# One PSUM bank for the last 64 columns of two token tiles

## The chip, the core and the metric

The kernel runs on one core of a Trainium2 chip. Its engines each work through a queue of their own: PE (TensorE, matmuls and turns, with its weight loads, PEld, shown apart), DVE (VectorE), ACT (ScalarE), POOL (GpSimd) and SP (SyncE, which here only starts DMAs). Matmuls write to PSUM, of which the kernel has eight banks of 128 partitions by 512 fp32 values. The metric is the device time of one execution in microseconds (us).

## What is computed

With B = 1, 2048 tokens, D = 576 channels, 128 states and a hidden width of 4608:

```python
xn = layernorm(x)                                # over the 576 channels
K  = Re(sum_n C[d,n] * exp(dt*A[d,n]*l) * dt*B[d,n])   # for l = 0..2047
y  = causal_conv(xn, K) + xn * Dskip             # by FFT in the reference
h  = silu(xn @ w1)                               # 576 -> 4608
out = x + y + h @ w2                             # 4608 -> 576
```

The feed-forward part (the two large products) and the convolution part share only `xn` and the final sum.

## The kernel before

**Tiles and staging.** The tokens are 16 tiles of 128. For the first product the channels must lie on partitions, so tiles 0 to 7 are turned on PE; tiles 8 to 15 are turned through DVE and memory instead. Four tiles make a block of 512 tokens. The product's accuracy comes from splitting each operand into a rounded part and the rest: a cast on ACT gives the high part, a subtraction on DVE the rest. A turned block is held as `xh` and `xl` (channels 0 to 511, four groups of 128) and `x4`, which holds the high part of channels 512 to 575 on partitions 0 to 63 and their rest on partitions 64 to 127.

**The turn of one tile** is `put_xt`. Four turns of 128x128 fill a PSUM bank `pt` (L124), one ACT cast makes `xh` (L125), one DVE subtraction `xl` (L126). Then a second bank is taken: one turn of the last 64 columns (L128), an ACT cast of 64x128 into the upper half of `x4` (L129), a DVE subtraction into its lower half (L130). The banks come from the pool `pss`, which has three and is shared with all of the convolution's work.

**Order of the feed-forward.** `up` makes one 128-wide slice of the hidden layer for 512 tokens: twelve matmuls with `xh` and `xl` (L314), and two with `x4` (L315, L316), into one of the two banks of `ps1`; then SiLU (L322) and a cast (L323) on ACT and a subtraction (L324) on DVE. `down` multiplies four such slices by `w2` into `po` (L339), and DVE adds the result to `acc` (L343). The first block's slices are made in two halves of 256 tokens: the first after tiles 0 and 1, the second after tiles 2 and 3. Weights are loaded by SP and split like the rest (L281 and L283 for `w1`, L300 and L302 for `w2`).

**Order of the side work.** `phase0` loads, normalizes and turns tiles 0 and 1 one by one, 2 and 3, 4 and 5, 6 and 7 as pairs. `norm` takes statistics (L187, L188), an inverse root on POOL (L192) and scales on DVE (L196) or ACT (L201). `late` does tiles 8 to 15 in a buffer that the next pair reuses: after normalizing (`xj`), DVE turns 32x32 blocks (L240), SP writes them (L244), and SP writes `xj` itself to `dxn` (L245). Then come the convolution's parameters (`natural`, with three changes of the activation table on ACT), its kernel, its transforms, and at the end its sum into the output.

**What sets the order on an engine.** The program is traced in the order of the code, and a planner then orders each engine's queue by estimated times, trace order and free banks; that order is fixed before the kernel runs. `behind(pins[...])` forces instructions traced inside it to stand behind the named one on the same engine. Of the pins, `xt_h` is the last large cast, `xt_s` the last cast into `x4`, `xt_v` the last subtraction into `x4`, and `pt` the last short turn. `xt0s` (tile 0) and `xt1s` (tile 1) hold back the first casts of `w1`; `xt1`, `xt3` and `xt7` hold back DVE work behind the named tile's last subtraction; the first `w2` casts stand behind `xt_s`. While PE waits for tiles 0 and 1, it runs filler matmuls (`idle`, L858, eight after tile 0 and three after tile 1), pinned behind `pt`.

Of the kernel before, what the change touches and what calls it, by code (L numbers as in the profile page):

```python
# [19 lines left out]
P = 128  # L20
L = 2048
D = 576
# [3 lines left out]
NKT = 4  # L26
# [17 lines left out]
def kernel(  # L44
# [21 lines left out]
    nc = tc.nc  # L66
# [23 lines left out]
    ident = cst.tile([P, P], F32, name="ident")  # L90
# [23 lines left out]
    def new_xt(blk):  # L114
        xh = xtp.tile([P, NKT, 512], F32R, tag="xh", name=f"xh_{blk}")
        xl = xtp.tile([P, NKT, 512], F32R, tag="xl", name=f"xl_{blk}")
        x4 = xtp.tile([P, 512], F32R, tag="x4", name=f"x4_{blk}")
        return xh, xl, x4

    def put_xt(xh, xl, x4, src):  # L120

        pt = pss.tile([P, NKT, P], F32, tag="pss", name="pt")
        for kt in range(NKT):
            nc.tensor.transpose(pt[:, kt, :], src[:, kt * P:(kt + 1) * P], ident)  # L124
        pins["xt_h"] = nc.scalar.copy(xh, pt).ins  # L125
        nc.vector.tensor_sub(xl, pt, xh)  # L126
        pt = pss.tile([P, 512], F32, tag="pss", name="pt4")
        pins["pt"] = nc.tensor.transpose(pt[:64, :P], src[:, NKT * P:D], ident).ins  # L128
        pins["xt_s"] = nc.scalar.copy(x4[:64, :], pt[:64, :P]).ins  # L129
        pins["xt_v"] = nc.vector.tensor_sub(x4[64:, :], pt[:64, :P], x4[:64, :]).ins  # L130

    xts = {}
    pairs = {}
    pins = {}

    def behind(ins):
        return tc.issue_after(ins) if ins is not None else nullcontext()
# [24 lines left out]
    def load_x(j, pool, tag, engines):  # L162

        t = pool.tile([P, 2, D], F32, tag=tag, name=f"{tag}{j}")
        for i in range(2 if j == 0 else 1):
            for ps, v, eng in quarters(xv, engines):
                if j:
                    eng.dma_start(t[ps], v[:, j:j + 2])
                else:
                    eng.dma_start(t[ps, i], v[:, i])  # L170
        pairs[j] = t
        return t[:, 0, :], t[:, 1, :]
# [7 lines left out]
    def norm(p0, js, xs):  # L180

        n = len(js)
        st = p0.tile([P, 2, 2, 6], F32, tag="st", name="st")
        mv = p0.tile([P, 2, 2], F32, tag="mv", name="mv")
        for i in range(n):
            for h in range(2):
                nc.vector.bn_stats(out=st[:, i, h, :], in_=xs[i][:, h * HD:(h + 1) * HD])  # L187
            nc.vector.bn_aggr(out=mv[:, i, :], in_=st[:, i, :, :])  # L188
        sd = p0.tile([P, 2], F32, tag="sd", name="sd")
        mb = p0.tile([P, 2], F32, tag="mb", name="mb")  # L190
        pins["sdv"] = nc.vector.tensor_scalar(sd[:, :n], mv[:, :n, 1], 1e-5, None, op0=ALU.add).ins
        pins["sd"] = nc.gpsimd.tensor_tensor(sd[:, :n], sd[:, :n], mhalf[:, :n], op=ALU.pow).ins  # L192
        xn = p0.tile([P, 2, D], F32, tag="xn", name="xn") if js[0] < 8 else pairs[js[0]]
        for i, j in enumerate(js):
            if j % 2 == 0 or j < 4:
                pins["xn"] = nc.vector.tensor_scalar(xn[:, i, :], xs[i], mv[:, i, 0:1], sd[:, i:i + 1],  # L196
                                                 op0=ALU.subtract, op1=ALU.mult).ins
            else:
                nc.vector.scalar_tensor_tensor(mb[:, i:i + 1], mv[:, i, 0:1], -1.0, sd[:, i:i + 1],
                                               op0=ALU.mult, op1=ALU.mult)  # L200
                nc.scalar.activation(xn[:, i, :], xs[i], AF.Identity,  # L201
                                     scale=sd[:, i:i + 1], bias=mb[:, i:i + 1])
        return xn

    def phase0(p0, js, idle=None):

        xs = load_x(js[0], accp, "acc", (nc.sync, nc.scalar) if js[0] < 2 else (nc.sync,))
        acc.update(zip(js, xs))
        yield
        if js[0]:  # L210
            with behind(pins["w1l"] if js[0] == 2 else None):
                normed(p0, js, xs)
        else:
            for j, xj in zip(js, xs):
                with behind(pins["xn"] if j else None):
                    normed(p0, (j,), (xj,))
                if not j:
                    pins["xt0s"] = pins["xt_s"]
                with behind(pins["pt"]):
                    idle(3 if j else 8)  # L220
        pins[f"xt{js[1]}h"] = pins["xt_h"]
        pins[f"xt{js[1]}"], pins[f"xt{js[1]}s"] = pins["xt_v"], pins["xt_s"]
        yield

    def normed(p0, js, xs):
        xn = norm(p0, js, xs)
        for i, j in enumerate(js):
            b, jj = divmod(j, 4)
            if b < 2:
                if jj == 0:  # L230
                    xts[b] = new_xt(b)
                c = slice(jj * P, (jj + 1) * P)
                xh, xl, x4 = xts[b]
                put_xt(xh[:, :, c], xl[:, :, c], x4[:, c], xn[:, i, :])
        if js[0] >= 8:

            b, jj = divmod(js[0], 4)
            tr = p0.tile([P, 2, D], F32, tag="tr", name="tr")
            for i in range(2):
                nc.vector.transpose(tr[:, i, :], xn[:, i, :])  # L240
            for q in range(4):
                cols = dxt[b - 2][:, jj * P:(jj + 2) * P].rearrange("(k r) (i q c) -> q r i k c", r=32, i=2, q=4)[q]
                for i in range(2):
                    nc.sync.dma_start(cols[:, i], tr[32 * q:32 * q + 32, i].rearrange("r (k c) -> r k c", c=32))  # L244
        nc.sync.dma_start(dxn[:, js[0]:js[0] + len(js)], xn[:, :len(js)])  # L245
# [596 lines left out]
    def side():  # L842
# [3 lines left out]
        with tc.tile_pool(name="kf", bufs=1) as kfp:  # L846
            for n in ("f", "phi"):
                kf[n] = kfp.tile([P, D], F32, name=n + "T")
            with tc.tile_pool(name="par", bufs=1) as par:
                with tc.tile_pool(name="pa", bufs=4) as pa:  # L850

                    zero = pa.tile([P, 512], BF16, name="zero", bufs=1)
                    nc.vector.memset(zero, 0.0)
                    pz = ps1.tile([P, 512], F32, tag="ps1", name="pz")

                    def idle(n):
                        for _ in range(n):
                            nc.tensor.matmul(pz, zero[:, :P], zero, start=True, stop=True)  # L858

                    idle(12)  # L860
                    p01, p23 = phase0(pa, (0, 1), idle), phase0(pa, (2, 3))
                    next(p01)
                    yield 0
                    next(p23)
                    next(p01)
                    yield 0
                    yield 0
                    next(p23)
                    yield 0
                    for js in ((4, 5), (6, 7)):  # L870
                        with behind(pins["xt3" if js[0] == 4 else "w2l"]):
                            for _ in phase0(pa, js):
                                pass
                    kf["dt"] = steps()
                    for n, ap in (("are", a_re), ("aim", a_im)):
                        kf[n] = par.tile([96, 6, NS], F32, tag=n, name=n)
                        nc.sync.dma_start(kf[n], ap.rearrange("(p t) n -> p t n", t=6))
                    yield 0
                with tc.tile_pool(name="nat", bufs=1) as nat, tc.tile_pool(name="pb", bufs=1) as pb:
                    nt = natural(nat, par)  # L880
                    def late(j):

                        xs = load_x(j, pb, "xj", (nc.sync,))
                        yield
                        with behind(pins["xn" if j == 8 else "gl"]):
                            normed(pb, (j, j + 1), xs)
                        yield

                    tiles = chain.from_iterable(late(j) for j in range(8, NJ, 2))
                    for at, todo in ((0.0, nt), (0.0, tiles), (0.004, tiles), (0.005, tiles), (gate_of(0), nt), (0.026, tiles), (0.028, tiles), (0.036, tiles), (0.038, tiles), (gate_of(1), nt), (0.06, tiles), (gate_of(2), nt), (0.09, nt)):  # L890
                        yield at
                        with behind(pins["gl"] if at else pins["xt7"] if todo is nt else None):
                            next(todo, None)
# [108 lines left out]
```

## Time and profile before

| | |
|---|---|
| time, median of 3 runs | 1112.2 us (1112.11 to 1112.43) |
| profiled execution, its own time | 1112.55 us |
| its span in the profile | 1110.8 us |
| granted TensorE clock | 0.999 |
| busy: PE, weight loads, DVE, ACT | 1103.5, 998.1, 917.3, 708.0 us |
| turned tiles: first and last short turn (L128) | 7.36 and 42.31 us |

In rows of the profile, `L128` is a line of the kernel, `pt<-ident,xn` names what is written and read, and `x8` is a count. A timeline row begins with start and duration in us; brackets give the idle time before it and what ended it. In rows of groups the busy time and the mean duration in ns follow the first bar. The chain that ended last is followed back from the last instruction, at each step to what released it; its rows have start, duration, engine, tile and line. A PE record's end is modelled, and records of successive matmuls overlap.

### The profile page before, as it was taken

Reading aid. Unit: us, or ns where it says so; the run is one execution under the profiler, and the core shown is the slowest. Engines: PE = TensorE matmul, PEld = TensorE weight load, DVE = VectorE, ACT = ScalarE, POOL = GpSimd, SP = SyncE. Lnnn points to the kernel's source line nnn. Section 1 sums busy time; section 2 is a strip of 40 time slices with the busy share of each in tenths; the row PEclk is TensorE's granted clock in tenths of the full one; section 3 lists DMA queues with packets and bytes.
Section 4 is the critical chain, followed back from the end, with each engine's and each line's share of the span. In section 5 each row is a group of like instructions: output and inputs, shape, how many; then the busy total and the mean of one; then the engine's idle time right before and its main releaser. Section 6 shows DMA issues by size and latency. Waiting matters only on the chain.

```text
span 1110.8 us, 22919 instructions
## 1 busy us (share of the span) xinstructions
PE 1103.5 (99%) x9167; PEld 998.1 (90%) x9167; DVE 917.3 (83%) x1546; ACT 708.0 (64%) x1227; POOL 70.8 (6%) x127
## 2 busy tenths in 40 slices
PE   9999999999999999999999999999999999999998
PEld 6888999899889899899989989999999999999887
DVE  7799899999999999999999837787778778784433
ACT  4574456676777676677866536877777778774210
POOL 1101000000000000011000000000000000000111
PEclk9999999999999999999999999999999999999999
DMA  9745521425242515255834163554544445434973
GB/s 255 204 123 152 140 69 61 120 65 128 82 107 81 133 61 131 76 158 155 217 124 105 44 177 102 168 158 129 161 143 151 140 147 169 131 107 129 255 207 86
DMA packets 175851, 148.56 MB, mean 134 GB/s; under 512 B 111088, under 2 KB 142720, under 8 KB 175616
## 3 DMA queue, kind: packets, MB, share of 16 engines
q1 hardware_dynamic: 165408, 112.69, 38.0%
q0 software_dynamic: 9504, 33.49, 9.4%
q8 instruction: 72, 1.18, 0.5%
q10 hardware_dynamic: 832, 0.92, 0.3%
q14 instruction: 35, 0.29, 0.1%
HBM read 102.53 MB, written 44.61 MB: 132 GB/s over the span
## 4 chain that ended last, share of the span: by engine, by line
PE 94%; DMA 2%; DVE 1%; ACT 1%; SPq 1%; issue 0%; POOL 0%; DVEq 0%; ACTq 0%
PE po L339 40%; PE ph L314 34%; PE kp L675 3%; PE ph L315 3%; PE ph L316 3%; PE pu L805 2%; PE pb L805 2%; PE pk L805 2%; PE z L690 2%; PE pu L155 1%; PE py L826 1%; PE pu L156 1%; DMA acc<-in_A_u_dram 1%; DMA dxn<-xj 1%; DMA w1r<-in_B_w_dram 0%; DMA xj<-in_A_u_dram 0%
## 5 line engine op out<-in xcount | busy, mean ns | idle before, releaser
L339 PE MATMUL po<-w2l,gh 128*128 128x288 f32 x1152 | 339.3, 296 | 0.0
L339 PE MATMUL po<-w2h,gl 128*128 128x288 f32 x1152 | 336.9, 295 | 0.0
L339 PE MATMUL po<-w2h,gh 128*128 128x288 f32 x1152 | 336.1, 296 | 0.0
L339 PEld LDWEIGHTS po<-w2h,gh 128*128 128x128 f32 x1152 | 215.3, 188 | 7.5 <-issue 2.8
L339 PEld LDWEIGHTS po<-w2l,gh 128*128 128x128 f32 x1152 | 216.2, 188 | 5.1 <-issue 0.5
L339 PEld LDWEIGHTS po<-w2h,gl 128*128 128x128 f32 x1152 | 215.7, 188 | 0.8
L322 ACT ACTIVATE gf<-ph 128x512 f32<-128x512 f32 (+1 forms) x148 | 86.3, 584 | 142.8 <-PE ph L316 133.6
L314 PE MATMUL ph<-xh,w1h 128*128 128x512 f32 (+1 forms) x592 | 161.8, 388 | 0.7 <-ACT xh L125 0.6
L314 PE MATMUL ph<-xl,w1h 128*128 128x512 f32 (+1 forms) x592 | 161.7, 386 | 0.2 <-DVE xl L126 0.2
L314 PE MATMUL ph<-xh,w1l 128*128 128x512 f32 (+1 forms) x592 | 161.2, 386 | 0.6 <-DVE w1l L283 0.6
L343 DVE TENSOR_TENSOR acc<-po,acc 128x288 f32<-128x288 f32 x288 | 126.4, 451 | 37.8 <-PE po L339 36.3
L324 DVE TENSOR_TENSOR gl<-gf,gh 128x512 fp32r<-128x512 f32 (+1 forms) x148 | 99.0, 672 | 64.3 <-ACT gh L323 63.5
L314 PEld LDWEIGHTS ph<-xh,w1l 128*128 128x128 f32 x592 | 108.1, 188 | 20.9 <-DVE w1l L283 1.1
L314 PEld LDWEIGHTS ph<-xl,w1h 128*128 128x128 f32 x592 | 108.1, 188 | 20.5 <-DVE xl L126 0.7
L314 PEld LDWEIGHTS ph<-xh,w1h 128*128 128x128 f32 x592 | 104.5, 188 | 17.8 <-ACT xh L125 1.2
L323 ACT CAST gh<-gf 128x512 fp32r<-128x512 f32 (+1 forms) x148 | 89.5, 608 | 10.1 <-PE po L339 7.2
L632 ACT ACTIVATE c<-th,magic 128x1040 f32<-128x1040 f32 x36 | 42.1, 1169 | 37.8 <-DVE C L655 27.9
L634 ACT ACTIVATE c<-th 128x1040 f32<-128x1040 f32 x36 | 38.7, 1075 | 33.9 <-DVE th L633 33.8
L300 ACT CAST w2h<-w2r 128x576 fp32r<-128x576 f32 x72 | 47.0, 671 | 17.3 <-PE po L339 14.9
L283 DVE TENSOR_TENSOR w1l<-w1r,w1h 128x640 fp32r<-128x640 f32 x72 | 57.0, 817 | 0.2
L316 PE MATMUL ph<-x,w1l 128*128 128x512 f32 (+1 forms) x148 | 57.0, 386 | 0.0
L315 PE MATMUL ph<-x,w1h 128*128 128x512 f32 (+1 forms) x148 | 57.0, 385 | 0.0
(182 smaller groups left out, 1830.4 us busy)
## 6 DMA issues: line engine op xcount, KB each, us to landing
w2r<-in_B_w_dram SPq DMA_DIRECT2D x72, 288.0 KB, 3.9
w1r<-in_B_w_dram SPq DMA_DIRECT2D x35, 512.0 KB, 3.7
d1u<-u POOLq DMA_DIRECT2D x32, 288.0 KB, 2.4
d1k<-stage SPq DMA_DIRECT2D x18, 512.0 KB, 6.9
ur<-d1u SPq DMA_DIRECT2D x32, 288.0 KB, 3.9
kr<-d1k SPq DMA_DIRECT2D x32, 288.0 KB, 2.7
d<-yo POOLq DMA_DIRECT2D x32, 288.0 KB, 3.2
ys<-d SPq DMA_DIRECT2D x32, 288.0 KB, 11.3
```

The source lines that it names most:

```text
L283: pins["w1l"] = nc.vector.tensor_sub(l1, src, h1).ins
L300: pins["w2h"] = nc.scalar.copy(h2, r2).ins
L314: nc.tensor.matmul(ph, w[:, kt, :], v[:, kt, a:e], start=n + kt == 0, stop=False)
L315: nc.tensor.matmul(ph, h1[:, 4, :], x4[:, a:e], start=False, stop=False)
L316: pins["pe"] = nc.tensor.matmul(ph, l1[:, 4, :], x4[:, a:e], start=False, stop=True).ins
L322: nc.scalar.activation(gf, ph, AF.Silu)
L323: pins["gh"] = nc.scalar.copy(gh, gf).ins
L324: pins["gl"] = nc.vector.tensor_sub(gl, gf, gh).ins
L339: pins["pe"] = nc.tensor.matmul(po[:, :HD], G[blk, t][g][:, js], W2[half, c, t][w][:, hs], start=n == 0, stop=n == 3 * FT - 1).ins
L343: nc.vector.tensor_add(acc[j][:, hs], po[:, :HD], acc[j][:, hs])
L632: nc.scalar.activation(c65, th, AF.Identity, bias=magic)
L805: nc.tensor.matmul(dst, st, mv[:, hs], start=n == 0, stop=n == 3 * len(terms) - 1)
```

## The change

`put_xt` loses its second half. A new function `put_x4` turns the last 64 columns of two tiles into one bank, side by side, and then makes one cast and one subtraction of 64x256 for both. `normed` keeps the tiles in a list and calls `put_x4` after each odd tile, so tile 0's short turn follows tile 1's large ones, and likewise for 2 and 3, 4 and 5, 6 and 7. The pin `pt` now also names a large turn (for the eight fillers after tile 0), and `xt0s` names tile 0's large cast.

```diff
-    def put_xt(xh, xl, x4, src):
+    def put_xt(xh, xl, src):
         pt = pss.tile([P, NKT, P], F32, tag="pss", name="pt")
         for kt in range(NKT):
-            nc.tensor.transpose(pt[:, kt, :], src[:, kt * P:(kt + 1) * P], ident)
+            pins["pt"] = nc.tensor.transpose(pt[:, kt, :], src[:, kt * P:(kt + 1) * P], ident).ins
         pins["xt_h"] = nc.scalar.copy(xh, pt).ins
         nc.vector.tensor_sub(xl, pt, xh)
+
+    def put_x4(x4, srcs):
         pt = pss.tile([P, 512], F32, tag="pss", name="pt4")
-        pins["pt"] = nc.tensor.transpose(pt[:64, :P], src[:, NKT * P:D], ident).ins
-        pins["xt_s"] = nc.scalar.copy(x4[:64, :], pt[:64, :P]).ins
-        pins["xt_v"] = nc.vector.tensor_sub(x4[64:, :], pt[:64, :P], x4[:64, :]).ins
+        for i, src in enumerate(srcs):
+            pins["pt"] = nc.tensor.transpose(pt[:64, i * P:(i + 1) * P], src[:, NKT * P:D], ident).ins
+        pins["xt_s"] = nc.scalar.copy(x4[:64, :], pt[:64, :2 * P]).ins
+        pins["xt_v"] = nc.vector.tensor_sub(x4[64:, :], pt[:64, :2 * P], x4[:64, :]).ins
...
                 if not j:
-                    pins["xt0s"] = pins["xt_s"]
+                    pins["xt0s"] = pins["xt_h"]
...
-                put_xt(xh[:, :, c], xl[:, :, c], x4[:, c], xn[:, i, :])
+                put_xt(xh[:, :, c], xl[:, :, c], xn[:, i, :])
+                lasts.append(xn[:, i, :])
+                if jj % 2:
+                    put_x4(x4[:, (jj - 1) * P:(jj + 1) * P], lasts)
+                    lasts.clear()
```

More of the change, by code (lines that the diff above doesn't have):

```diff
@@ L118, in new_xt @@
         return xh, xl, x4
-    def put_xt(xh, xl, x4, src):
+    def put_xt(xh, xl, src):
         pt = pss.tile([P, NKT, P], F32, tag="pss", name="pt")
         for kt in range(NKT):
-            nc.tensor.transpose(pt[:, kt, :], src[:, kt * P:(kt + 1) * P], ident)
+            pins["pt"] = nc.tensor.transpose(pt[:, kt, :], src[:, kt * P:(kt + 1) * P], ident).ins
         pins["xt_h"] = nc.scalar.copy(xh, pt).ins
         nc.vector.tensor_sub(xl, pt, xh)
+    def put_x4(x4, srcs):
         pt = pss.tile([P, 512], F32, tag="pss", name="pt4")
-        pins["pt"] = nc.tensor.transpose(pt[:64, :P], src[:, NKT * P:D], ident).ins
-        pins["xt_s"] = nc.scalar.copy(x4[:64, :], pt[:64, :P]).ins
-        pins["xt_v"] = nc.vector.tensor_sub(x4[64:, :], pt[:64, :P], x4[:64, :]).ins
+        for i, src in enumerate(srcs):
+            pins["pt"] = nc.tensor.transpose(pt[:64, i * P:(i + 1) * P], src[:, NKT * P:D], ident).ins
+        pins["xt_s"] = nc.scalar.copy(x4[:64, :], pt[:64, :2 * P]).ins
+        pins["xt_v"] = nc.vector.tensor_sub(x4[64:, :], pt[:64, :2 * P], x4[:64, :]).ins
     xts = {}
     pairs = {}
+    lasts = []
     pins = {}
```

## The prediction

> **What bounds the kernel now.** I read the page's busy shares and the chain that ended last first, then the waits of PE, then the chain in order of time, then the timelines of PE, DVE and ACT in the first 75 us. The change lives between 6 and 44 us.
>
> ```profile
> PE 1103.5 (99%) x9167; PEld 998.1 (90%) x9167; DVE 917.3 (83%) x1546; ACT 708.0 (64%) x1227; POOL 70.8 (6%) x127
> PE 94%; DMA 2%; DVE 1%; ACT 1%; SPq 1%; issue 0%; POOL 0%; DVEq 0%; ACTq 0%
> ```
>
> PE (the matmul engine) carries 94% of the chain. The change leaves the number of PE instructions alone (eight short turns before, eight after), so it can only pay or cost through PE's waits. The waits of PE, longest in total first:
>
> ```profile
> PE ph L314 <- DVE w1l L283: 0.6, 1, 0.6
> PE ph L314 <- ACT xh L125: 0.6, 1, 0.6
> PE ph L314 <- DVE xl L126: 0.2, 1, 0.2
> ```
>
> All three lie below 44 us, where the turned tiles are made: 1.4 us together. A very short wait does not show here, because matmul records overlap (below, one begins at 7.36 and lasts 0.27, and the next begins at 7.47). The chain in order of time shows one more, and shows that PE does not carry the chain early on:
>
> ```profile
> 36.64 0.46 DVE acc L343
> 37.10 0.49 DVE xj L196
> 37.74 0.88 ACT xj L201
> 38.64 0.78 DVE tr L240
> ...
> 44.73 6.06 DMA dxn<-xj
> ...
> 52.10 3.23 DMA xj<-in_A_u_dram
> ...
> 63.83 0.86 ACT xj L201
> ...
> 74.50 0.61 ACT gf L322
> ...
> 75.15 3.01 PE ph L314 x12
> ```
>
> From 37 to 75 us the chain is not PE. It is the normalization of tiles 8 and 9 on DVE, their write to memory, the reload of the same buffer with tiles 10 and 11, their normalization, an activation sequence on ACT, and the SiLU that frees a bank for PE at 75.15. From there to the end every longer piece is PE, at one pace from early to late:
>
> ```profile
> 368.13 3.18 PE po L339 x24
> ...
> 1031.63 2.72 PE ph L314 x12
> ```
>
> 3.18/24 is 0.1325 us for a `po` matmul, 2.72/12 is 0.227 us for a `ph`. So what counts is when PE gets past 75.15. Whatever is won before is kept only if this second chain moves too.
>
> **The change, part by part.** *Smaller work.* Four groups of two casts (ACT) and two subtractions (DVE) of 64x128 become four of 64x256. Their rows, and the nearest forms of other widths:
>
> ```profile
> L129 ACT CAST x<-pt x8: 243/258/259, 8.0 to 43.0; 64x128 fp32r<-64x128 f32 x8
> L130 DVE TENSOR_TENSOR x<-pt,x x8: 283/284/286, 9.6 to 43.9; 64x128 fp32r<-64x128 f32 x8
> ...
> L729 ACT COPY ka<-pk 64x288 f32<-64x288 f32 x64 | 25.1, 392 | 15.4 <-PE pk L805 14.5
> L736 DVE TENSOR_TENSOR y<-pu,kb 64x288 f32<-64x288 f32 x64 | 29.4, 459 | 1.4
> ```
>
> No row has 64x256. It lies between the 128 and the 288 columns, close to the latter: on a straight line 258+(392-258)x128/160 = 365 ns on ACT and 284+(459-284)x128/160 = 424 ns on DVE. Per pair that saves 2x258-365 = 151 ns and 2x284-424 = 144 ns, over four pairs 0.6 us on each. The bounds are those of the two forms: from 2x284-459 = 109 ns to 284 ns per pair on DVE. Both engines work beside PE, so nothing of this is in the sum by itself; if the cover went, it would be worth at most those 0.6 us.
>
> *Tiles 0 and 1.* One short turn moves from before the eight filler matmuls to after tile 1's turns, and the first weight cast on ACT need only follow the large cast.
>
> ```profile
> 7.36 0.27 PE L128 MATMUL pt<-ident,xn 128*64 128x128 f32 x1
> 7.47 1.89 PE L858 MATMUL pz<-zero 128*128 128x512 bf16 x8
> 9.20 0.60 PE L124 MATMUL pt<-ident,xn 128*128 128x128 f32 x4
> ...
> 16.87 0.75 PE L314 MATMUL ph<-xh,w1l 128*128 128x256 f32 x4 [0.62 <-DVE w1l L283]
> ```
>
> The fillers start 7.47-7.36 = 0.11 us earlier, and so may tile 1's turns. At 16.87 PE waits 0.62 us for a weight split on DVE. That split stands behind tiles 2 and 3's statistics, which wait for a load:
>
> ```profile
> 14.00 1.54 DVE L187 BATCH_NORM_STATS2 st<-acc 128x6 f32<-128x288 f32 x4 [0.94 <-DMA acc<-in_A_u_dram]
> 15.99 0.82 DVE L283 TENSOR_TENSOR w1l<-w1r,w1h 128x640 fp32r<-128x640 f32 x1
> ```
>
> None of the merged work stands between 14.00 and 16.8, so the 0.11 us only lengthens the wait: 0. Bounds: from 0.11 won to 0.14 lost (the longer merged subtraction ahead of the first weight split, hidden by the same 0.62).
>
> *Tiles 2 and 3.* Here the merged work is on PE's path:
>
> ```profile
> 20.52 0.28 DVE L130 TENSOR_TENSOR x<-pt,x 64x128 fp32r<-64x128 f32 x1
> 20.83 0.69 DVE L126 TENSOR_TENSOR xl<-pt,xh 128x512 fp32r<-128x512 f32 x1
> ...
> 21.08 0.27 PE L128 MATMUL pt<-ident,xn 128*64 128x128 f32 x1
> 21.58 0.74 PE L314 MATMUL ph<-xl,w1h 128*128 128x256 f32 x4 [0.23 <-DVE xl L126]
> ```
>
> Tile 2's short subtraction stands directly ahead of tile 3's `xl`, for which PE waits at 21.58. It moves behind it, so `xl` starts 20.83-20.52 = 0.31 us earlier and PE can go on near 21.27. The short turn at 21.08 waited for a bank; with three banks for two large turns and one shared short one, the pair can stand before 19.3. Even both at 21.0 (2x0.11 us) end before 21.27. Late next are the second-layer weights, cast on ACT behind the x4 cast:
>
> ```profile
> 21.39 0.26 ACT L129 CAST x<-pt 64x128 fp32r<-64x128 f32 x1 [0.29 <-PE pt L128]
> 21.55 2.39 ACT L300 CAST w2h<-w2r 128x576 fp32r<-128x576 f32 x4
> ...
> 23.66 0.74 DVE L302 TENSOR_TENSOR w2l<-w2r,w2h 128x576 fp32r<-128x576 f32 x1
> 24.47 0.39 PE L339 MATMUL po<-w2l,gh 128*128 128x288 f32 x1
> ```
>
> With the turns early the merged cast leaves the place at 21.39, and the `w2h` casts start up to 0.4 us earlier; with the turns at 21.0 the merged cast delays them by about 0.2. `w2l` ends at 24.40, right ahead of its use at 24.47. DVE saves only 0.31-0.45+0.31 = 0.17 us up to there (a short subtraction takes 0.31 of the queue, as 20.52 to 20.83 shows; the merged one some 0.45). So PE keeps between 0.17 and 0.31 us; I take 0.2. Lower bound: with the late turns 0.2 us lost.
>
> *Tiles 4 to 7.* The short turns no longer compete for two banks of a pair. PE's wait is for tile 7:
>
> ```profile
> 41.87 0.60 PE L124 MATMUL pt<-ident,xn 128*128 128x128 f32 x4
> 43.15 2.11 PE L314 MATMUL ph<-xh,w1h 128*128 128x512 f32 x8 [0.56 <-ACT xh L125]
> ```
>
> If tile 7's turns come sooner, these 0.56 us go. But then PE meets the bank at 75.15 that much too early, so this part is 0 in the sum unless the other chain moves as well. That chain begins at a DVE wait for PE (0.41 us before the `acc` of 36.64), so the 0.2 us of tiles 2 and 3 do pass into it.
>
> No DMA is added, removed or given another source; the writes of `xn` hang on the normalization alone. Sum: 0 - 0.2 + 0 = -0.2 us. The profiled execution took 1112.55 us (span 1110.8 and 1.75 around it), so 1112.35; it stands 0.35 above the median of the runs, which makes 1112.0.
>
> **The rivals.** *The late tiles are pushed back (slower).* In the order before, tile 8's normalization (37.10) stands ahead of tile 6's subtractions on DVE:
>
> ```profile
> 40.10 0.69 DVE L126 TENSOR_TENSOR xl<-pt,xh 128x512 fp32r<-128x512 f32 x1
> ...
> 55.42 1.18 DVE L187 BATCH_NORM_STATS2 st<-xj 128x6 f32<-128x288 f32 x3 [1.92 <-DMA xj<-in_A_u_dram]
> 56.51 0.68 DVE L324 TENSOR_TENSOR gl<-gf,gh 128x512 fp32r<-128x512 f32 x1
> ```
>
> If freed banks let tiles 6 and 7 be turned sooner, the planner, which traced them first, puts their `xl` ahead of 37.10. Then the write at 44.73, the reload and the SiLU at 74.50 move back by as much: 0.69 for one, 0.69x2+0.42 = 1.8 for both with the merged subtraction. Two `acc` additions drawn along (0.46 each) make 2.7. Less the 0.2 won, the time is 1112.7 to 1114.7. It decides the sign from 0.2 us of displacement on, and exceeds the 0.2% from 2.4. For it: the chain has no slack at 75.15. Against it: the planner may still time tile 7 as late as 41.87.
>
> [...]
>
> *The gaps close (faster).* Tile 7's wait goes and the DVE chain moves up instead of back. Then the stall at the bank goes too, whose size comes from the matmuls before it:
>
> ```profile
> 73.95 1.07 PE L314 MATMUL ph<-xl,w1h 128*128 128x512 f32 x4
> ```
>
> 73.95 plus four of 0.227 is 74.86, so 0.29 up to 75.15. With PE's 0.31 and 0.56 that makes 1.16, and with the 0.6 us of DVE work at most 1.8. Time 1110.4 to 1111.0 (1112.2 less 1.8 and 1.16). Against it: the reload is bound by DMA pieces of 6.06 and 3.23 us that no cast shortens.
>
> *The plan changes further on.* Each queue's order is planned from estimated times; a shift of some tenths can reorder DVE and ACT behind 75 us. PE has no recorded wait there, so this mostly costs: a stall like those seen is 0.6 us, and four of them are 2.4, to 1114.6 or more.
>
> [...]
>
> *PE has room that its 99% hides (faster).* Weight loads are busy 998.1 of 1110.8 us, so 112.7 us could hold stalls that a new order would take out; 2% of it, 2.3 us, gives 1109.9. The trace speaks against it: `po` and `ph` keep the same pace at 368 and at 1031 as in the chain between, which is no row of stalls. It gets a chance of 0.06.
>
> *It does nothing.* If the planner leaves the pair where the second short turn stood, the time is 1112.2.
>
> **How the numbers follow.** 0.2% (2.2 us) is about what a measurement of this kernel can tell from no change. Forecast 0.28 and "it does nothing" 0.08, both between 1111.6 and 1112.6. Late tiles pushed back: 0.22, of which 0.07 over 2.2 us slower. Gaps close: 0.12, all within 2.2 us. Plan changes further on: 0.24, of which 0.18 over 2.2 us slower. Hidden room: 0.06, all over 2.2 us faster. So faster 0.06, same 0.69, slower 0.25. The range 1110.3 to 1116.0 leaves out the 0.06 below and about a tenth above.
>
> **What would show it.** L129 and L130 with four instructions each of 64x256, near 365 and 424 ns. No short subtraction ahead of tile 3's `xl`, and PE's wait of 0.23 us for `xl` gone or smaller. The wait for `w1l` near 16.9 kept, at 0.6 to 0.75 us. The order of tile 6's and 7's `xl` against tile 8's normalization decides between forecast and first rival: the write of `xj` at 44.5 or at 45.4 and later, and the `ph` of 75.15 at 74.9 or later than 75.3. From there to the end the distance should stay 1110.8-75.15 = 1035.6 us; if it grows by over 1 us, the third rival holds, and the prediction is wrong in its claim that PE's pace behind 75 us is untouched.

## The result, and the profile after

| | before | after |
|---|---|---|
| time, median of 6 runs each on one chip | 1112.15 us | 1122.74 us |
| lowest and highest | 1111.76, 1112.52 | 1121.13, 1125.57 |
| ratio to before | | 1.0092 [1.0082, 1.0103] |
| profiled execution, its own time and span | 1112.55, 1110.8 us | 1121.13, 1119.4 us |

The changed kernel is 0.9% slower, some 10 us. The range reached up to 1116.0, so the forecast failed in size and in sign. Its profiled execution is the fastest of the six; what the others have beyond it comes in the last section.

The busy line of the page looks as before:

```profile
PE 1104.4 (99%) x9167; PEld 997.5 (89%) x9167; DVE 916.8 (82%) x1542; ACT 708.3 (63%) x1223; POOL 73.4 (7%) x127
```

The same number of matmuls, four instructions fewer on DVE and on ACT. PE's busy share is no help: 99% both times. The groups of the changed lines have the sizes that were worked out:

```profile
L133 ACT CAST x<-pt x4: 365/365/367, 10.3 to 40.5; 64x256 fp32r<-64x256 f32 x4
L134 DVE TENSOR_TENSOR x<-pt,x x4: 418/418/420, 11.1 to 42.1; 64x256 fp32r<-64x256 f32 x4
```

So the edit does what it says, at 365 and 418 ns. The waits of PE are where the two kernels part (in total, count, longest):

```profile
PE po L348 <- DVE acc L352: 3.6, 4, 1.9
PE po L348 <- ACT w2h L309: 2.4, 2, 2.1
...
PE ph L323 <- DVE w1l L292: 0.7, 1, 0.7
...
PE py L835 <- DMA ys<-d: 0.5, 1, 0.5
```

The first two lines are new, 6.0 us together, and they do not lie in the first 75 us, where the edit is. The timeline after, at the places that the prediction named and at the first matmul of the convolution's end (`py`):

```profile
14.69 1.54 DVE L192 BATCH_NORM_STATS2 st<-acc 128x6 f32<-128x288 f32 x4 [1.55 <-DMA acc<-in_A_u_dram]
...
17.57 0.74 PE L323 MATMUL ph<-xh,w1l 128*128 128x256 f32 x4 [0.73 <-DVE w1l L292]
...
73.31 0.96 PE L323 MATMUL ph<-xh,w1h 128*128 128x512 f32 x3 [0.66 <-ACT gf L331]
...
1043.17 1.24 PE L835 MATMUL py<-ys,s 64*32 64x288 f32 x32 [0.50 <-DMA ys<-d]
```

and the answering row of before:

```profile
1034.73 1.23 PE L826 MATMUL py<-ys,s 64*32 64x288 f32 x32
```

The `ph` of 75.15 now begins at 73.31: the head is 1.84 us *ahead*. From there to `py` it was 1034.73-75.15 = 959.58 us and is 1043.17-73.31 = 969.86, so 10.28 are lost. From `py` to the end: 76.07 before, 76.23 after. Sum: -1.84+10.28+0.16 = 8.6, the difference of the spans. To place the loss, I took for each matmul the time from its start to the next start beyond the median for its kind (shapes and tiles), where that excess is over 0.1 us, and subtracted the same sum of before: 3.7 us from 100 to 160 us, 1.6 from 160 to 400, 2.5 from 400 to 600, 0.4 from 600 to 1030, 0.7 at `py`. That is 8.9 of the 10.3; the rest is spread in smaller pieces.

**The first stall, at 118 us, followed back.** After:

```profile
63.23 1.28 ACT L524 ACT_TABLE_LOAD   x1
...
68.47 0.87 ACT L206 ACTIVATE xj<-xj,mb,sd 128x576 f32<-128x576 f32 x1
...
74.17 2.55 SPq L253 DMA_DIRECT2D dxt<-tr  x4
76.76 3.26 SPq L173 DMA_DIRECT2D xj<-in_A_u_dram  x4
...
103.73 6.27 SPq L253 DMA_DIRECT2D dxt<-tr  x8
110.05 1.91 SPq L173 DMA_DIRECT2D xj<-in_A_u_dram  x4
...
114.97 1.54 DVE L192 BATCH_NORM_STATS2 st<-xj 128x6 f32<-128x288 f32 x4 [3.03 <-DMA xj<-in_A_u_dram]
...
117.75 0.45 DVE L352 TENSOR_TENSOR acc<-po,acc 128x288 f32<-128x288 f32 x1
...
118.25 0.40 PE L348 MATMUL po<-w2h,gh 128*128 128x288 f32 x1 [1.85 <-DVE acc L352]
...
141.93 0.06 DVE L591 MEMSET magic<- 128x1 f32 x1 [5.23 <-DMA dxt<-tr]
...
145.45 0.40 PE L348 MATMUL po<-w2h,gh 128*128 128x288 f32 x1 [0.84 <-DVE acc L352]
```

Before:

```profile
63.83 0.86 ACT L201 ACTIVATE xj<-xj,mb,sd 128x576 f32<-128x576 f32 x1
...
65.83 1.28 ACT L515 ACT_TABLE_LOAD   x1
...
69.88 1.85 SPq L168 DMA_DIRECT2D xj<-in_A_u_dram  x4
...
96.55 1.91 SPq L168 DMA_DIRECT2D xj<-in_A_u_dram  x4
...
103.53 1.53 DVE L187 BATCH_NORM_STATS2 st<-xj 128x6 f32<-128x288 f32 x4
```

Before, tile 11's scaling on ACT (63.83) stands ahead of the activation table's change (65.83). After, the change comes first (63.23) and the scaling behind it, at 68.47. The SiLU that the `ph` of 73.31 waits for starts at 72.67 in place of 74.50, but not by the swap: tile 11's scaling stands ahead of it on ACT in both kernels. What comes earlier is the step ahead of both, the activation of `ci` (60.08 in place of 63.08), with the DVE step that it waits for (59.14 in place of 62.09). The buffer's reload with tiles 12 and 13 moves from 69.88 to 76.76, that with tiles 14 and 15 from 96.55 to 110.05, and the statistics for these wait for data at 114.97, with 3.03 us of DVE idle. The addition that PE waits for (`acc` at 117.75) stands behind them on DVE. At 141.93 DVE has been idle for another 5.23 us, for the writes of these tiles' turned blocks, and the stall at 145 follows. What PE gains at 73.31 it pays back at 118 and 145. DVE's loss is seen in the windows (length, then PE, PEld, DVE, ACT and POOL busy, the clock and the DMA); 100 to 150 us before, and three stretches after:

```profile
100.00:150.00 50.00, 50.00 (x309) 45.83 (x308) 46.92 (x82) 22.01 (x35) 1.97 (x3) 1.00 0.48 140
```

```profile
100.00:150.00 50.00, 47.08 (x289) 42.16 (x287) 40.22 (x71) 17.22 (x28) 6.05 (x3) 1.00 0.59 161
150.00:400.00 250.00, 248.83 (x2610) 224.03 (x2611) 242.37 (x364) 171.79 (x254) 8.10 (x15) 1.00 0.35 91
400.00:600.00 200.00, 197.72 (x2035) 177.73 (x2035) 194.93 (x292) 140.59 (x214) 11.26 (x20) 1.00 0.47 129
```

**The stall at 450 us.** After:

```profile
444.90 1.42 DVE L311 TENSOR_TENSOR w2l<-w2r,w2h 128x576 fp32r<-128x576 f32 x2
...
445.68 1.00 SPq L300 DMA_DIRECT2D w2r<-in_B_w_dram  x2
...
449.17 0.67 ACT L309 CAST w2h<-w2r 128x576 fp32r<-128x576 f32 x1 [3.20 <-DMA w2r<-in_B_w_dram]
...
449.90 0.53 PE L348 MATMUL po<-w2h,gh 128*128 128x288 f32 x2 [2.14 <-ACT w2h L309]
```

Before:

```profile
438.93 1.42 DVE L302 TENSOR_TENSOR w2l<-w2r,w2h 128x576 fp32r<-128x576 f32 x2
...
439.71 1.00 SPq L291 DMA_DIRECT2D w2r<-in_B_w_dram  x2
...
442.67 0.68 ACT L300 CAST w2h<-w2r 128x576 fp32r<-128x576 f32 x1
```

Both kernels load a slice of `w2` right behind the subtraction that frees its buffer, 0.78 us after its start. The cast follows 3.74 us after that start before, 4.27 after. Before, PE has other `po` matmuls to run in the meantime; after, it runs out of them 2.08 us after the load's issue (449.90-2.14-445.68): the one that needs the slice comes earlier in its queue and waits 2.14 us.

### The profile page after: what moved, and what is told of

It is laid out like the page before. It is cut to its first block, busy times and chain, and to the rows that moved or that the text cites. A ratio compares the mean times of both kernels' runs of the same rounds, so it can differ in the third digit from the quotient of the medians.

```text
span 1119.4 us, 22904 instructions
## 1 busy us (share of the span) xinstructions
PE 1104.4 (99%) x9167; PEld 997.5 (89%) x9167; DVE 916.8 (82%) x1542; ACT 708.3 (63%) x1223; POOL 73.4 (7%) x127
## 4 chain that ended last, share of the span: by engine, by line
PE 68%; DVE 16%; issue 6%; ACT 4%; DMA 3%; SPq 1%; POOL 1%; DVEq 0%; ACTq 0%; POOLq 0%
PE po L348 29%; PE ph L323 24%; PE ph L324 2%; PE pu L814 2%; PE ph L325 2%; PE pk L814 2%; PE pb L814 2%; DVE acc L352 2%; PE kp L684 2%; DVE th L625 2%; DVE C L652 1%; DVE S L663 1%; DVE gl L333 1%; PE z L699 1%; DVE th L642 1%
## 5 line engine op out<-in xcount | busy, mean ns | idle before, releaser
L311 DVE TENSOR_TENSOR w2l<-w2r,w2h 128x576 fp32r<-128x576 f32 x72 | 53.6, 753 | 4.5 <-ACT w2h L309 4.3
```

The costliest lines, as they stand in the source:

```text
L311: pins["w2l"] = nc.vector.tensor_sub(l2, r2, h2).ins
```

## The experiments

The theory after the traces: the paired turn itself costs nothing; what costs is that it makes the planner order the queues anew, above all tile 11's scaling behind the table change. Rivals: the merged casts or the shared bank cost time themselves; any small edit of the head costs this much; the delay of DVE is carried along and makes the later stalls.

### Which tiles: the first four, or the last four

```diff
                 lasts.append(xn[:, i, :])
-                if jj % 2:
+                if not (j < 4):            # for the second run: (j >= 4)
+                    put_x4(x4[:, c], lasts)
+                    lasts.clear()
+                elif jj % 2:
                     put_x4(x4[:, (jj - 1) * P:(jj + 1) * P], lasts)
```

`put_x4` then takes as many columns as there are tiles in the list. In the second run `xt0s` names tile 0's short cast, as before.

> The changed kernel, but only tiles 0 to 3 share a bank in pairs; tiles 4 to 7 are turned and cast one by one as before. Theory A (the loss comes from the pairs 4 to 7, which move tile 11's normalization on ACT behind a change of the activation table, so the late tiles' loads and writes come late, DVE idles some 8 us between 100 and 145 us, and PE pays for it): 1110.5 to 1112.5, PE's waits for acc at 118 and 145 us gone. Rival B (the merged casts or the shared bank themselves cost, in proportion to the pairs): about half the loss, 1116 to 1118.

> The changed kernel, but only tiles 4 to 7 share a bank in pairs; tiles 0 to 3 as before. Theory A: 1118 to 1124, with DVE idle for the last late load or for the write of the late tiles, somewhere between 100 and 145 us. Rival B (cost in proportion to the pairs): 1116 to 1118. Rival C (any small edit moves the plan by as much): cannot be told here.

Only tiles 0 to 3 paired: 1111.76 us against 1112.95, ratio 0.9991 [0.9982, 1.0001]. Only tiles 4 to 7 paired: 1119.78, ratio 1.0054 [1.0032, 1.0075]. The window of the first, which may be laid beside those above:

```profile
100.00:150.00 50.00, 50.00 (x308) 45.83 (x307) 46.93 (x82) 22.28 (x36) 1.96 (x3) 1.00 0.47 136
```

PE is busy throughout (and for 250.00 and 200.00 us of the two next stretches), with nearly the counts of before. The planned queues say the same. The table has the lines by which the order of each engine's instructions differs from that of before (names and shapes compared, line numbers left out), for these and the later kernels. They were counted on the planned queues, which no profile holds. Counted on the profiled instructions, with equal neighbours merged, DVE has 38 and 79 lines for the two versions near the old order and 605 to 702 for the seven far from it, so the gap is the same:

| kernel | PE | DVE | ACT | SP | ratio |
|---|---|---|---|---|---|
| before, nine fillers | 2 | 0 | 0 | 2 | 0.9998 |
| before, late tiles ahead | 0 | 5 | 2 | 2 | 0.9993 |
| tiles 0 to 3 paired | 42 | 38 | 21 | 8 | 0.9988 |
| all paired, tile 11 on DVE | 89 | 79 | 33 | 12 | 1.0027 |
| tiles 4 to 7 paired | 1604 | 590 | 351 | 87 | 1.0054 |
| all paired, tiles 11 and 13 on DVE | 1571 | 582 | 326 | 70 | 1.0040 |
| all paired, late tiles ahead | 1714 | 611 | 365 | 65 | 1.0038 |
| all paired, late tiles ahead, `w2l` raised | 1740 | 640 | 377 | 66 | 1.0047 |
| before, ten comparisons more | 1857 | 634 | 418 | 89 | 1.0069 |
| all paired (the changed kernel) | 1650 | 632 | 347 | 102 | 1.0092 |
| all paired, separate casts | 1640 | 676 | 354 | 86 | 1.0093 |

So in the changed kernel it is the pairs 4 to 7 that bring a new order. By themselves they do not bring the stalls at 118 and 145: in the second run DVE is busy 46.49 us from 100 to 150 and PE all of it, while a stall at a load of `w2` is there, 2.26 us at 442.44. Tile 11's scaling (59.75) stands ahead of the table change (62.32) in it, and the reloads are early (66.08 and 91.36). So its time lies in the expected range, but not for the expected reason. Its profiled execution took 1115.23; what the median has beyond that comes in the last section too.

The first version once more, timed more often:

> Only tiles 0 to 3 paired, timed once more for a closer interval, since 0.9991 [0.9982, 1.0001] left open whether this version is better than the kernel before. Theory A (the paired turn itself costs nothing and pays a little at the head, 0.36 us at the wait for w1l, 0.23 at xl): 1111.5 to 1112.0, ratio 0.9990 to 0.9999, PE with no stall above 0.3 us from 75 us to the tail. Rival (no gain that can be measured): the ratio's interval holds 1.

1111.3 us (11 runs, 0.2 below the expected range) against 1112.58 (23 runs), ratio 0.9988 [0.9979, 0.9997]: it beats the kernel before by about 0.1%. The waits for `w1l` near 17 and for `xl` at 21.58 are gone.

### Tile 11 without ACT

```diff
-            if j % 2 == 0 or j < 4:
+            if j % 2 == 0 or j < 4 or j == 11:
                 pins["xn"] = nc.vector.tensor_scalar(xn[:, i, :], xs[i], ...
```

> The changed kernel with all four pairs, but tile 11 is normalized on DVE instead of ACT (0.58 us of DVE for 0.87 of ACT), so that its turning and the next late load no longer hang on ACT's queue. Theory A: the loss goes, 1110 to 1112.5, since the head is some 1.8 us ahead at 73 us; DVE's idle times of 3.0 and 5.2 us near 112 and 137 us are gone, and with them the stalls at 394 and 450 us. Rival B (merged casts cost): 1121 to 1123 stays. Rival D (the stalls near 394 and 450 us are reorderings of their own, not consequences): only some 3.5 us come back, 1117 to 1119.

1116.36 us, ratio 1.0027 [1.0017, 1.0037], so 7 us of the 10 are gone, and the time lies between the ranges of the expectation. Yet the early stall did not go, it moved forward. The timeline of this kernel:

```profile
93.22 0.86 ACT L206 ACTIVATE xj<-xj,mb,sd 128x576 f32<-128x576 f32 x1
...
101.76 1.90 SPq L173 DMA_DIRECT2D xj<-in_A_u_dram  x4
...
106.71 1.54 DVE L192 BATCH_NORM_STATS2 st<-xj 128x6 f32<-128x288 f32 x4 [4.94 <-DMA xj<-in_A_u_dram]
```

Now it is tile 13's scaling that stands late, behind three table changes (the last at 91.43). DVE loses 4.94 us here, and PE stalls four times from 110 to 121 us (3.6 us in all). But from 150 to 600 PE is busy all the time, 250.00 and 200.00 us. So here a delay of DVE at 100 to 120 us is not carried on into later stalls, and with the late tiles put ahead (below) later stalls come without such a delay; that rival falls. And this kernel has all four pairs with a planned order near that of before (79 lines on DVE): the pairs bring no cost of their own behind 150 us either.

Tiles 11 and 13 both on DVE (`j in (11, 13)`):

> The changed kernel with tiles 11 and 13 normalized by DVE and not ACT, so that no step of these tiles can stand behind a table change on ACT (DVE does 2 x 0.5 us more). Theory (the stalls at 118 and 145 us come from tile 11 behind the table change, and those of e3 at 110 to 120 from tile 13 behind it): PE has no stall over 0.5 us from 76 to 160 us, DVE is busy over 45 us of 100 to 150, and the time is 1113.5 to 1116.5. Rival (the reload is late for another reason, SP's queue of weight loads ahead of it): stalls of 1 us or more between 105 and 150 us stay, and the time is 1117 or more.

No stall over 0.2 us from 76 to 160 us, DVE 46.30 us busy from 100 to 150, the reload of tiles 14 and 15 at 96.17: this part is as the theory has it. The median is not: 1118.24 us, ratio 1.004 [1.0023, 1.0057]. Three of the six runs, at a granted clock of 0.999 or 1.000, took 1114.82 to 1116.41, as expected; the other three, at 0.996 to 0.998, took 1120.07 to 1120.90. In the profiled execution (1120.9) there are in place of the early stalls one of 2.20 us for a `w2h` at 506.16 and one of 3.23 for a load (`ys`) at 1041.50.

### A small edit elsewhere

```diff
-                    idle(3 if j else 8)
+                    idle(3 if j else 9)
```

> The kernel before with nine filler matmuls after tile 0 instead of eight: an edit of 0.2 us at 8 us that touches nothing else. Theory A: the order of the late tiles stays, so 1111.5 to 1113. Rival C (any small edit shifts the plan by per cents): 1115 or more, or under 1109.

The kernel before with one more filler matmul: 1112.9 against 1112.95 us, 0.9998 [0.9989, 1.0007], with the order as it was. Not every edit of the head moves it.

### The late tiles put ahead

```diff
-                        with behind(pins["xn" if j == 8 else "gl"]):
+                        with tc.high_priority(), behind(pins["xn" if j == 8 else "gl"]):
                             normed(pb, (j, j + 1), xs)
```

In the changed kernel, and then in the kernel before as a control:

> The changed kernel with all four pairs, and the normalization of tiles 8 to 15 traced with high priority, so that the planner puts each step of it as early as it is ready; tile 11's step on ACT then stands ahead of the first change of the activation table and tile 13's between the next two, as in the kernel before. Theory A (late tiles): the loss goes, 1110 to 1113, with no PE stall at 110 to 150 us and DVE idle under 4 us from 100 to 150. Rival D (the stall for a second-layer weight near 440 to 450 us has a cause of its own): 1113 to 1115 with that stall kept at 2.3 us. Rival B (merged casts cost by themselves): 1121 to 1123.

> The kernel before with the priority of e5_late_first alone: tiles 8 to 15's normalization is put ahead where the planner has a choice. The control for e5. Theory (e5 won its 6.5 us by putting the late tiles' chain back where the kernel before has it): here the priority finds that order in place already, PE's order is the same, so the time is that of the kernel before within 0.15% (1111 to 1114) and PE has no stall between 76 and 600 us. Rival (the priority is worth something of its own in any order): 2 us or more faster, below 1110.5.

The changed kernel with it: 1116.2 us, ratio 1.0038 [1.0025, 1.0051], so 1.0092-1.0038 = 0.54% or 6 us less than without, yet between the ranges of the expectation (up to 1115, and from 1121). The kernel before with it: 1111.93, ratio 0.9993 [0.9984, 1.0002], with PE's order unchanged. The timeline and the waits of the first:

```profile
62.04 0.85 ACT L206 ACTIVATE xj<-xj,mb,sd 128x576 f32<-128x576 f32 x1
...
64.04 1.28 ACT L524 ACT_TABLE_LOAD   x1
...
68.20 1.85 SPq L173 DMA_DIRECT2D xj<-in_A_u_dram  x4
```

```profile
PE py L835 <- DMA ys<-d: 3.0, 1, 3.0
...
PE pu L160 <- ACT stage L707: 1.0, 1, 1.0
PE po L348 <- ACT gh L332: 0.8, 1, 0.8
PE po L348 <- ACT w2h L309: 0.8, 1, 0.8
```

Tile 11's scaling is ahead of the table change again, the reloads are at 68.20 and 94.93, and nothing stalls from 60 to 150 us. So with all four pairs in place the early stalls come from the order of the late tiles, and putting these ahead is worth about 6 of the 10 us. Not all of the 6 is this one chain: the early stretch was 3.7 us of the loss, and the order further on has changed too (no stall at 450). What is left sits in the waits of the second fence, all of them behind 380 us; they are 5.6 us together in this profiled execution, which took 1118.51.

### Separate casts in the shared bank

```diff
-        pins["xt_s"] = nc.scalar.copy(x4[:64, :], pt[:64, :2 * P]).ins
-        pins["xt_v"] = nc.vector.tensor_sub(x4[64:, :], pt[:64, :2 * P], x4[:64, :]).ins
+        for c in (slice(0, P), slice(P, 2 * P)):
+            pins["xt_s"] = nc.scalar.copy(x4[:64, c], pt[:64, c]).ins
+            pins["xt_v"] = nc.vector.tensor_sub(x4[64:, c], pt[:64, c], x4[:64, c]).ins
```

> The changed kernel with the shared bank and the moved turns of all four pairs, but two casts and two subtractions of 64x128 per pair, as before. Theory A: the sizes of the casts don't matter, the order does; tile 11's step again stands behind the change of the table, and tile 13's behind the next ones, so 1116 to 1123 with PE waiting for DVE at 105 to 150 us. Rival B (the merged form costs): 1112 to 1113.

1122.85 us, ratio 1.0093 [1.0078, 1.0108]. The casts are as small as before and the time is that of the changed kernel; tile 11's scaling stands behind the table change here too (66.46 and 63.04). The merging of the casts is not what costs.

### DVE made busier

Ten more copies of one comparison (L552) in the kernel before, 5.4 us of DVE near 125 us:

```diff
         v.tensor_scalar(rc, pi, 0.0, None, op0=ALU.is_lt)
+        v.tensor_scalar(rc, pi, 0.0, None, op0=ALU.is_lt)   # ten times
```

> The kernel before with one DVE instruction of the parameter stage (0.54 us, comparing pi with zero) done eleven times instead of once, 5.4 us of DVE work near 125 us. If DVE is the true bound up to 600 us, as its 97% there suggests: 1116 to 1118.5. If PE is the bound and DVE has room: 1112 to 1114, unless the planner's order changes in a way that stalls PE, which its waits would show.

1120.04 us, ratio 1.0069 [1.005, 1.0088], outside both expected ranges. No stall from 100 to 370 us, so the added work was hidden where it stands; but for one of 0.79 at 25.02, the new stalls lie behind 380 us, the longest 1.68 us at 573.04 for a `w2h`, with DVE *less* busy from 400 to 600 us (188.57 us) than before (193.41). The edit was meant to show whether DVE's load sets the later stalls. It changed the planned order as well, so it doesn't tell that. What it does show is that the later stalls can come with no pair in the kernel at all; how much of the nearly 8 us (1120.04 against 1112.31) is the order's and how much the added work's is not separated.

### The later stalls

```diff
-            with behind(pins["w1l"] if first else None):
+            with tc.high_priority() if not first else nullcontext(), behind(pins["w1l"] if first else None):
                 pins["w2l"] = nc.vector.tensor_sub(l2, r2, h2).ins
```

First with tiles 4 to 7 paired alone, to have the `w2` buffer freed sooner; then with all pairs and the late tiles put ahead.

> Pairs of tiles 4 to 7 alone, as in the run with 1119.8, and the subtraction for the second-layer weights on DVE with high priority, so that their buffer comes free and the next load starts sooner. Rival D (the stall of 2.4 us at 442 us comes from that load, which waits for the subtraction): the stall goes, 1112 to 1116. If the load is not held by the subtraction: 1118 to 1121 with the stall kept.

> e5_late_first with the subtraction of the second layer's weights raised as well, in all blocks but the first: the same pairs and the same priority for the late tiles, but another order behind 100 us on PE, ACT and DVE. Theory D (what e5 has left, about 3.9 us, is not in the pairs but in which weight load, cast or table step the planner happened to set late between 370 and 600 us and at the tail): no stall over 1 us between 76 and 370 us, the stalls at 383.06 (0.94), 563.96 (1.00) and 568.65 (1.14) are gone or elsewhere, and the time moves by more than 1 us against e5, to 1112.5 to 1115 if the order is better, 1117.5 to 1121 if it is worse. Rival (a fixed cost that the pairs of tiles 4 to 7 carry): the same 1116.2 within 0.8, with the stalls at the same places.

The first: 1119.67 us, ratio 1.0053 [1.0036, 1.0071]. The subtraction kept its place, the stall stayed (2.31 us at 442.62), so the edit separated nothing. The second: 1118.31 us, ratio 1.0047 [1.0033, 1.0062], about a us worse than with the late tiles ahead alone, and the two intervals overlap. Its one run at a granted clock of 1.000 took 1116.11, no more than those of the other (1115.58 to 1116.85 at 0.999 and 1.000), so it does not tell a fixed cost from an order's. The stalls at 384 (0.9 us) and 568 (0.6) are still where they were, the one at 563.96 is gone, and a new one of 1.49 us stands at 25.23. The expectation of gone or moved stalls held for one of three. Some stalls are common to several new orders; but tile 11 on DVE, with all the pairs, has none of them.

**What stays open.** That a new order makes the stalls from 380 us on is shown in two ways: all the pairs with nearly the old order have none there (tile 11 on DVE), and the kernel before, without a pair, has them with a new order (ten comparisons, with their own work beside it). Which step of the new order makes each of them, about 4 us together, is not settled; at 450 us it is the place of one `po` in PE's queue. Nor do the runs show which of the planner's estimates tips tile 11's scaling behind the table change.

## Why the prediction was wrong

*Sizes.* 365 ns was forecast for the cast and 365 measured; 424 and 418 for the subtraction. Right, and worth nothing by itself, as said.

*Tiles 0 and 1: 0.* The wait for `w1l` is kept, 0.73 us, as forecast. The matmul behind it starts 0.70 us later (17.57 against 16.87), beyond the bound of 0.14: the load of `acc` that the statistics wait for landed later, at 14.69 instead of 14.00. That load was in the working as the cover, but not as something that can move.

*Tiles 2 and 3: -0.2.* PE's wait for `xl` is gone, as forecast. The first use of `w2l` came at 24.54 in place of 24.47, so of the 0.70 lost before all but 0.07 was won back. Right in kind; the 0.63 is above the 0.31 that was the most.

*Tiles 4 to 7: 0.* Wrong. The wait for tile 7 went, and the second chain did move: the SiLU of 74.50 starts at 72.67. The head won 1.84 us, about what the rival "gaps close" had as its most (1.8); the agreement is luck in part, since the stall at the bank, one of its terms, stayed (0.66 us).

*The late tiles pushed back.* Not in the way described: the reload of the first late buffer came at 49.49 instead of 50.81. The late chain was hit one pair further on, at tile 11, on ACT and not on DVE, and not before 75 us but with its price at 118 and 145.

*PE's pace behind 75 us is untouched.* **This is the step that failed.** The text set a test: from the `ph` of 75.15 to the end 1035.6 us, and over 1 us more would mean that the third rival holds. It became 1119.4-73.31 = 1046.1. So the third rival held, with 10 us and not 2.4. The sum had no term for it: it took "PE has no recorded wait there" as a margin for the forecast, when that is a property of one order of the queues. The rival had the direction right ("this mostly costs"), but was given 0.24, and its price was put together from the stalls of the head (four of 0.6 us). The stalls that came were 2.14, 1.85, 0.84 and a number of smaller ones: what is waited for here is a load, 3.74 to 4.27 us from subtraction to cast, and not one instruction. It was the rival to be worked out from rows. The reload of tiles 14 and 15 is issued at 96.55 and its statistics start at 103.53, 6.98 us later; after, the same takes 114.97-110.05 = 4.92 with DVE waiting. So the chain had some 2 us of slack, and tile 11's scaling moved by 68.47-63.83 = 4.64. On the way the delay grew: 6.88 us at the reload of tiles 12 and 13, 9.92 at tile 12's scaling on DVE (97.84 against 87.92), 13.50 at the reload of tiles 14 and 15. Tile 11's step begins it and is not the whole of it.

*Room that the 99% hides, and "does nothing".* Neither. No run shows the 2.3 us, nor that the time without weight loads is room (1110.8-998.1 = 112.7 us before, 1119.4-997.5 = 121.9 after): no version gained more than 0.12%. And the pair of tiles 6 and 7 is turned at 39.86, between the places of the two single turns.

## What to carry to other kernels

Where a planner orders the queues, the first question to an edit is how much of the planned order changes, engine by engine, and only then what the edited instructions cost: here 38 changed lines on DVE went with 0.999, 79 with 1.003, and some 600 with 1.004 to 1.009 (a warning and not a price, since among the large counts the time does not follow the count). A profile with no waits on the bounding engine says that this one order has none; the slack of each load that lands ahead of its use (reload, landing, first use) has to be read from the rows before a new order is priced. And such an edit can be taken where the order stays (tiles 0 to 3 here) and left out where it doesn't.

## What the runs showed of the hardware

A stall of PE can cost more than its length. In the kernel with tiles 11 and 13 on DVE, PE idles 2.20 us at 506.16, and then the `po` matmuls follow each other at 0.24 us and not 0.13:

```profile
506.16 0.53 PE L348 MATMUL po<-w2h,gh 128*128 128x288 f32 x2 [2.20 <-ACT w2h L309]
...
509.55 0.45 PE L348 MATMUL po<-w2l,gh 128*128 128x288 f32 x1
509.79 0.41 PE L348 MATMUL po<-w2h,gl 128*128 128x288 f32 x1
```

From 506.4 to 510.0 fifteen starts come 1.6 us late in sum; the granted clock is 0.50 from 506.6 to 510.0 us, and 0.89 over 500 to 515. The same follows the 3.23 us at 1041.50 in this kernel, and the 3.0 at `py` with the late tiles put ahead (0.24 us from start to start, and a granted clock of 0.94 over 1030 to 1060 us, in both). It is not a matter of the idle time alone. With tiles 4 to 7 paired, without and then with the raised subtraction, the same matmul waits as long, and only the second time is the pace halved:

```profile
442.44 0.54 PE L352 MATMUL po<-w2h,gh 128*128 128x288 f32 x2 [2.26 <-ACT w2h L313]
442.81 0.29 PE L352 MATMUL po<-w2l,gh 128*128 128x288 f32 x1
442.94 0.29 PE L352 MATMUL po<-w2h,gl 128*128 128x288 f32 x1
```

```profile
442.62 0.53 PE L352 MATMUL po<-w2h,gh 128*128 128x288 f32 x2 [2.31 <-ACT w2h L313]
...
443.49 0.45 PE L352 MATMUL po<-w2l,gh 128*128 128x288 f32 x1
443.73 0.45 PE L352 MATMUL po<-w2h,gl 128*128 128x288 f32 x1
```

What differs between the two traces is where the idle time lies. The traces record the granted clock with its changes. Between the start and the end of a span each stretch of 0.50 lasts 3.41 us, and the stretches of full clock between two of them are whole multiples of that (532.48 us, 156 times, in the kernel with tiles 11 and 13 on DVE; 600.75, 176 times, with the raised subtraction). So in these traces the clock changes on a grid of 3.41 us, whose place differs from one execution to the next. The 2.31 us of idle lie whole in the step of the grid from 439.83 to 443.24, and the low clock begins at its end. The 2.26 us are cut at 441.10 into 0.92 and 1.34, and the clock stays (1.00 over 400 to 600 us). Over the spans of all 14 profiles, each step with 2.10 us of idle PE or more (five of them) was followed by a step at half clock, one of four with 1.64 to 1.68 us was (the stall of 1.68 at 573.04 with ten comparisons), and none with 1.56 or less.

This goes with the spread of the runs. The six runs of the changed kernel, by granted clock: 0.999 and 1.000 with spans of 1119.4 and 1119.8 us, 0.998 with 1120.8 and 1121.2, 0.996 with 1122.4 and 1123.8. The profiled run is the first of these and its record has no step at half clock behind a stall, so its 8.6 us are stalls, and the median's 10.6 hold some lowered clock beside them (1122.74-1121.13 = 1.6). One step at half clock lowers the mean clock of such a span by 0.0015 (0.5x3.41/1119), so 0.998 to 0.996 would be one to three of them; the runs that were not profiled don't show it. The kernel before, which has no such stall, stays at 0.999 or above in all its runs.

The other medians hold lowered clocks too. At 0.999 or above, the least time was 1111.7 us in the kernel before, 1114.82 to 1116.11 in the six versions that lack the early stalls or the later ones (tiles 4 to 7 paired, without and with the raised subtraction; tile 11, or 11 and 13, on DVE; late tiles ahead, without and with the raised subtraction), 1117.32 with ten comparisons, and 1121.13 in the changed kernel. So at the full clock it loses some 9 us, of which these versions take back 5.0 to 6.3.
